# A gated feed-forward kernel on one core: the first loads in two rounds, and 256 rows of gate ahead of the later transposes

## Chip, cores, metric

One core of a Trainium2 chip. The time is that of the device for one execution, in microseconds; the profile's span runs from the first to the last instruction and is about 1.3 us shorter. A run is called slow when it is over 1.5% above the fastest of its kernel, and only the others, the fast runs, enter a ratio. All times below are counted from the first instruction of the execution, unless another start is named.

## The reference

```python
B, S, D, F = 1, 2048, 640, 1536          # all bf16
def reference(x, w_gate, w_up, w_down):
    g = silu(x @ w_gate)
    u = x @ w_up
    return (g * u) @ w_down
```

## The kernel before

The kernel gives the array (TensorE) both operands with the contracted dimension on the partitions, so x has to be transposed. Rows are worked in blocks of 512 (four chunks of 128), and the columns of gate and up in slices of 128. The first 512 rows of x are loaded as they are and transposed on the array itself, through PSUM, by an identity matrix; the other rows are transposed by a DMA, much later. Only the start of the kernel matters here.

```python
queues = (nc.sync, nc.scalar)                       # SP queue, ACT queue
halves = ((0, KD // 2 + 1), (KD // 2 + 1, KD))      # contracted chunks 0..2 on SP, 3..4 on ACT
for c in (0, 1):                                    # x: chunks 0, 1 on SP, 2, 3 on ACT
    for i, eng in enumerate(queues):
        load_x(eng, c + 2 * i, c + 2 * i + 1)
for dst, src in ((wg_sb, wg_v), (wu_sb, wu_v)):     # first slice of gate, then of up
    for eng, (k0, k1) in zip(queues, halves):
        eng.dma_start(out=dst[:, k0:k1, wslice(0, 1)], in_=src[:, k0:k1, wslice(0, 1)])
load_w(nc.sync, wg_sb, wg_v, *W_CHUNKS[1])          # next gate slice: columns 128..383
nc.scalar.activation(silu_first[:], ones[:, 0:1], ACT.Silu)     # brings the table load early
load_w(nc.sync, wu_sb, wu_v, *W_CHUNKS[1])          # next up slice
# ... all other weights, then the DMA transposes of the later rows ...
```

The loads share eight DMA semaphores (eight numbers in the trace), so the ninth load waits until one of the first eight has landed: it is issued at 2.88, just behind the landing at 2.87. The first slice is worked by itself:

```python
h = (SUB - 1) * P                                   # 384 rows
warm(N_WARM)                                        # 20 matmuls on ones
for n, c in enumerate((0, 2, 1)):
    transpose_chunk(c, [(nc.vector.tensor_copy, ("po_a", "po_b")[n % 2], 0, KD)])
transpose_chunk(SUB - 1, [(nc.vector.tensor_copy, "po_b", 0, 2), (nc.scalar.copy, "po_a", 2, KD)])
warm(2)
proj(pg, wg_sb, fc, sb, 0, h)                       # gate, 384 rows
proj(pg, wg_sb, fc, sb, h, S_BLK)                   # gate, 128 rows
proj(pu, wu_sb, fc, sb, 0, S_BLK)                   # up, 512 rows
```

`proj` is five matmuls, one for each contracted chunk of 128; `transpose_chunk` is five transposes and the copies out of PSUM. Then come silu on ScalarE and the product on VectorE, and eleven more slices in the same manner with 512 rows at a time.

Of the kernel before, what the change touches and what calls it, by code (L numbers as in the profile page):

```python
# [10 lines left out]
def _body(  # L11
# [8 lines left out]
    nc = tc.nc  # L20
    P = nc.NUM_PARTITIONS
# [5 lines left out]
    B, S0, D = x.shape  # L27
    F = w_gate.shape[1]
    S = B * S0
# [3 lines left out]
    KD = D // P  # L33
    KF = F // P
    S_BLK = 512
    NSB = S // S_BLK
    SUB = S_BLK // P
    DA = 512
    Q = 32
    N_WARM = 20  # L40
    W_CHUNKS = [(0, 1), (1, 3), (3, 6), (6, 9), (9, 12)]
    assert D % P == 0 and F % P == 0 and S % S_BLK == 0 and D > DA and SUB >= 2

    consts = ctx.enter_context(tc.tile_pool(name="consts", bufs=1))
    work = ctx.enter_context(tc.tile_pool(name="work", bufs=3))
# [8 lines left out]
    wg_sb = consts.tile([P, KD, F], bf16)  # L54
    wu_sb = consts.tile([P, KD, F], bf16)
# [7 lines left out]
    wg_v = w_gate.rearrange("(kd p) f -> p kd f", p=P)  # L63
    wu_v = w_up.rearrange("(kd p) f -> p kd f", p=P)
    wd_v = w_down.rearrange("(kf p) d -> p kf d", p=P)

    def wslice(a, b):
        return slice(a * P, b * P)

    def load_w(eng, dst, src, a, b):  # L70
        eng.dma_start(out=dst[:, :, wslice(a, b)], in_=src[:, :, wslice(a, b)])

    def load_x(eng, c0, c1):
        eng.dma_start(out=x_sb[:, c0:c1, :], in_=x_v[:, c0:c1, :])  # L74
# [4 lines left out]

    queues = (nc.sync, nc.scalar)  # L80
    halves = ((0, KD // 2 + 1), (KD // 2 + 1, KD))
    for c in (0, 1):
        for i, eng in enumerate(queues):
            load_x(eng, c + 2 * i, c + 2 * i + 1)
    for dst, src in ((wg_sb, wg_v), (wu_sb, wu_v)):
        for eng, (k0, k1) in zip(queues, halves):
            eng.dma_start(out=dst[:, k0:k1, wslice(0, 1)], in_=src[:, k0:k1, wslice(0, 1)])
    load_w(nc.sync, wg_sb, wg_v, *W_CHUNKS[1])
    nc.scalar.activation(silu_first[:], ones[:, 0:1], ACT.Silu)  # L89
    load_w(nc.sync, wu_sb, wu_v, *W_CHUNKS[1])  # L90
    for a, b in W_CHUNKS[2:]:
# [9 lines left out]
    def warm(n):  # L101
        for _ in range(n):
            nc.tensor.matmul(  # L103
                pw[:, 0:P], lhsT=ones[:], rhs=ones[:], start=True, stop=True
            )

    def keep_order(engine):

        traced = [i for i in nc.cur_bb.bb.instructions if i.engine == engine]
        for a, b in zip(traced, traced[1:]):  # L110
            tc.add_manual_dep(
                b,
                a.name,
                mybir.DependencyInfo(
                    mybir.DependencyClass.NoSync, mybir.DependencyReason.DATA
                ),
                reason="keep_order",
            )

    def transpose_chunk(c, parts):  # L120
        c_sl = slice(c * P, (c + 1) * P)
        for copy, tag, k0, k1 in parts:
            pt = psum.tile([P, k1 - k0, P], bf16, tag=tag, name="pt")
            for kd in range(k0, k1):
                nc.tensor.transpose(  # L125
                    out=pt[:, kd - k0, :],
                    in_=x_sb[:, c, kd * P : (kd + 1) * P],
                    identity=ident[:],
                )
            copy(out=xT[:, k0:k1, c_sl], in_=pt[:])  # L130

    def proj(ps, w_sb, fc, sb, c0, c1):
        for kd in range(KD):
            nc.tensor.matmul(  # L134
                ps[:, c0:c1],
                lhsT=w_sb[:, kd, fc * P : (fc + 1) * P],
                rhs=xT[:, kd, sb * S_BLK + c0 : sb * S_BLK + c1],
                start=(kd == 0),
                stop=(kd == KD - 1),
            )  # L140

    for sb in range(NSB):
        s_sl = slice(sb * S_BLK, (sb + 1) * S_BLK)
        for fc in range(KF):
            pg = psum.tile([P, S_BLK], f32, tag="gu", name="pg", bufs=4)
            pu = psum.tile([P, S_BLK], f32, tag="gu", name="pu", bufs=4)
            if sb == 0 and fc == 0:
                h = (SUB - 1) * P
                warm(N_WARM)
                for n, c in enumerate((0, 2, 1)):  # L150
                    transpose_chunk(
                        c, [(nc.vector.tensor_copy, ("po_a", "po_b")[n % 2], 0, KD)]
                    )
                transpose_chunk(
                    SUB - 1,
                    [
                        (nc.vector.tensor_copy, "po_b", 0, 2),
                        (nc.scalar.copy, "po_a", 2, KD),
                    ],
                )  # L160
                warm(2)
                proj(pg, wg_sb, fc, sb, 0, h)
                proj(pg, wg_sb, fc, sb, h, S_BLK)
                proj(pu, wu_sb, fc, sb, 0, S_BLK)
                keep_order(mybir.EngineType.PE)
                keep_order(mybir.EngineType.Activation)
            else:
                proj(pg, wg_sb, fc, sb, 0, S_BLK)
                proj(pu, wu_sb, fc, sb, 0, S_BLK)
            sg = work.tile([P, S_BLK], f32)  # L170
            nc.scalar.activation(sg[:], pg[:], ACT.Silu)  # L171
            nc.vector.tensor_tensor(  # L172
                out=aT[:, fc, s_sl], in0=sg[:], in1=pu[:], op=ALU.mult
            )


        n_t = (SUB if sb < NSB - 1 else SUB - 1) * P
        po_t = psum.tile([P, n_t], f32, tag="po_b", name="po_t")
        for kf in range(KF):
            nc.tensor.matmul(  # L180
                po_t[:],
                lhsT=wd_sb[:, kf, DA:D],
                rhs=aT[:, kf, sb * S_BLK : sb * S_BLK + n_t],
                start=(kf == 0),
                stop=(kf == KF - 1),
            )
        ot_t = outp.tile([P, n_t], bf16, name="ot_t")
        ot_q = outp.tile([P, n_t], bf16, name="ot_q")
        nc.scalar.copy(ot_t[:], po_t[:])  # L189
        nc.vector.transpose(out=ot_q[:], in_=ot_t[:])  # L190
        for q in range(P // Q):
            nc.scalar.dma_start(
                out=out2[
                    sb * S_BLK : sb * S_BLK + n_t, DA + q * Q : DA + (q + 1) * Q
                ].rearrange("(i r) c -> r i c", r=Q),
                in_=ot_q[q * Q : (q + 1) * Q, :].rearrange("r (i c) -> r i c", c=Q),
            )

        for j in range(SUB):
            s0 = sb * S_BLK + j * P  # L200
            last = sb == NSB - 1 and j == SUB - 1
            po_a = psum.tile([P, DA], f32, tag="po_a", name="po_a")
            for kf in range(KF):
                nc.tensor.matmul(  # L204
                    po_a[:],
                    lhsT=aT[:, kf, s0 : s0 + P],
                    rhs=wd_sb[:, kf, 0:DA],
                    start=(kf == 0),
                    stop=(kf == KF - 1),
                )  # L210
            ot = outp.tile([P, DA], bf16, name="ot")
            nc.scalar.copy(ot[:], po_a[:])  # L212
            nc.sync.dma_start(out=out2[s0 : s0 + P, 0:DA], in_=ot[:])
            if last:
                po_b = psum.tile([P, D - DA], f32, tag="po_b", name="po_b")
                for kf in range(KF):
                    nc.tensor.matmul(  # L217
                        po_b[:],
                        lhsT=aT[:, kf, s0 : s0 + P],
                        rhs=wd_sb[:, kf, DA:D],  # L220
                        start=(kf == 0),
                        stop=(kf == KF - 1),
                    )
                ot_b = outp.tile([P, D - DA], bf16, name="ot_b")
                nc.vector.tensor_copy(out=ot_b[:], in_=po_b[:])  # L225
                nc.scalar.dma_start(out=out2[s0 : s0 + P, DA:D], in_=ot_b[:])
# [76 lines left out]
def kernel(tc, *args):  # L303
    _body(tc, *args)
    tc.close()
    tc.compile()
    _trim(tc.nc)
# [30 lines left out]
```

## Time and profile before

| | before |
|---|---|
| time, median of 6 runs | 164.01 us (163.91 to 164.37) |
| time of the profiled execution | 164.41 us |
| span of the profiled execution | 163.1 us |
| first useful matmul (gate) | 5.39 us |
| second column slice begins | 7.56 us |

In a timeline line the columns are start, duration, engine, line of the kernel, operation, output<-inputs, shape, count, and in brackets how long the engine was idle and what ended that. In a DMA line the last number is the time from issue to landing; issue time plus that is when the waiting engine may go on. The lines are in the prediction.

### The profile page before, as it was taken

Reading aid. Unit: us, or ns where it says so; the run is one execution under the profiler, and the core shown is the slowest. Engines: PE = TensorE matmul, PEld = TensorE weight load, DVE = VectorE, ACT = ScalarE, POOL = GpSimd, SP = SyncE. Lnnn points to the kernel's source line nnn. Section 1 sums busy time; section 2 is a strip of 40 time slices with the busy share of each in tenths; the row PEclk is TensorE's granted clock in tenths of the full one; section 3 lists DMA queues with packets and bytes.
Section 4 is the critical chain, followed back from the end, with each engine's and each line's share of the span. In section 5 each row is a group of like instructions: output and inputs, shape, how many; then the busy total and the mean of one; then the engine's idle time right before and its main releaser. Section 6 shows DMA issues by size and latency. Waiting matters only on the chain.

```text
span 163.1 us, 1864 instructions
## 1 busy us (share of the span) xinstructions
PE 159.1 (98%) x764; PEld 75.2 (46%) x779; DVE 37.8 (23%) x58; ACT 42.2 (26%) x71; POOL 0.6 (0%) x6
## 2 busy tenths in 40 slices
PE   8899999999999999999999999999999999999994
PEld 7544444444444444444444444444444444445442
DVE  2323333310013333311003333331001333332000
ACT  3222222212232222221222222221214222222121
POOL 1000000000000000000000000000000000000000
DMA  7999999803200000003110000000320000000312
GB/s 212 274 333 330 361 245 187 152 6 60 67 32 0 0 0 0 4 0 34 64 64 0 2 4 0 0 0 3 62 68 32 0 0 0 0 0 4 54 34 72
DMA packets 26888, 11.26 MB, mean 69 GB/s; under 512 B 17664, under 2 KB 26880, under 8 KB 26880
## 3 DMA queue, kind: packets, MB, share of 16 engines
q1 hardware_dynamic: 17968, 10.16, 22.9%
q10 hardware_dynamic: 8912, 0.98, 3.9%
q8 instruction: 6, 0.10, 0.3%
q14 instruction: 2, 0.02, 0.0%
HBM read 6.55 MB, written 2.62 MB: 56 GB/s over the span
## 4 chain that ended last, share of the span: by engine, by line
PE 95%; DMA 2%; issue 1%; DVE 0%; SPq 0%
PE pg L134 32%; PE pu L134 31%; PE po_a L204 25%; PE po_t L180 6%; DMA x_sb<-in_x_dram 2%; PE po_b L217 0%; PE pt L125 0%; DVE xT L130 0%; SPq L74 0%; DVE ot_b L225 0%
## 5 line engine op out<-in xcount | busy, mean ns | idle before, releaser
L134 PE MATMUL pg<-xT,wg_sb 128*128 128x512 bf16 (+2 forms) x245 | 59.7, 375 | 0.2 <-DVE xT L130 0.2
L134 PE MATMUL pu<-xT,wu_sb 128*128 128x512 bf16 x230 | 59.0, 379 | 0.5
L172 DVE TENSOR_TENSOR aT<-sg,pu 128x512 bf16<-128x512 f32 x48 | 33.0, 687 | 100.8 <-PE pu L134 100.8
L171 ACT ACTIVATE sg<-pg 128x512 f32<-128x512 f32 x48 | 28.7, 597 | 71.1 <-PE pg L134 71.1
L204 PE MATMUL po_a<-wd_sb,aT 128*128 128x512 bf16 x188 | 41.9, 379 | 0.2
L134 PEld LDWEIGHTS <-wg_sb 128*128 128x128 bf16 x245 | 23.8, 98 | 28.4 <-DMA wg_sb<-in_w_gate_dram 0.4
L134 PEld LDWEIGHTS <-wu_sb 128*128 128x128 bf16 x240 | 23.4, 98 | 28.1
L204 PEld LDWEIGHTS <-aT 128*128 128x128 bf16 x192 | 18.8, 98 | 22.5
L212 ACT CAST ot<-po_a 128x512 bf16<-128x512 f32 x16 | 9.4, 585 | 32.4 <-PE po_a L204 19.2
L180 PE MATMUL po_t<-aT,wd_sb 128*128 128x512 bf16 (+1 forms) x47 | 10.3, 366 | 0.1
L180 PEld LDWEIGHTS <-wd_sb 128*128 128x128 bf16 x48 | 4.7, 98 | 5.1
L189 ACT CAST ot_t<-po_t 128x512 bf16<-128x512 f32 (+1 forms) x4 | 2.2, 558 | 11.6 <-PE po_t L180 11.6
L190 DVE STREAM_TRANSPOSE ot_q<-ot_t 128x512 bf16<-128x512 bf16 (+1 forms) x4 | 2.7, 678 | 9.1 <-ACT ot_t L189 9.1
L103 PE MATMUL pw<-ones 128*128 128x128 bf16 x22 | 2.6, 302 | 0.4 <-DVE ones L78 0.4
L225 DVE CAST ot_b<-po_b 128x128 bf16<-128x128 f32 x1 | 0.3, 292 | 9.9 <-PE po_b L217 9.9
L125 PE MATMUL pt<-ident,x_sb 128*128 128x128 bf16 x20 | 2.0, 269 | 0.5 <-DMA x_sb<-in_x_dram 0.5
L130 DVE COPY xT<-pt 128x640 bf16<-128x640 bf16 (+1 forms) x4 | 1.7, 439 | 3.5 <-PE pt L125 3.5
L103 PEld LDWEIGHTS <-ones 128*128 128x128 bf16 x22 | 2.2, 139 | 0.4 <-DVE ones L78 0.4
L125 PEld LDWEIGHTS <-x_sb 128*128 128x128 bf16 x20 | 1.6, 122 | 0.9 <-DMA x_sb<-in_x_dram 0.8
L89 ACT ACT_TABLE_LOAD x1 | 1.3, 1283 | 2.0 <-issue 2.0
L130 ACT COPY xT<-pt 128x384 bf16<-128x384 bf16 x1 | 0.5, 479 | 1.6 <-PE pt L125 1.6
L217 PEld LDWEIGHTS <-aT 128*128 128x128 bf16 x12 | 0.8, 98 | 0.2
(9 smaller groups left out, 2.1 us busy)
## 6 DMA issues: line engine op xcount, KB each, us to landing
out_dram<-ot SPq DMA_DIRECT2D x16, 128.0 KB, 1.7
wd_sb<-in_w_down_dram SPq DMA_DIRECT2D x1, 1920.0 KB, 11.8
wg_sb<-in_w_gate_dram SPq DMA_DIRECT2D x3, 480.0 KB, 7.1
wu_sb<-in_w_up_dram SPq DMA_DIRECT2D x3, 480.0 KB, 7.8
out_dram<-ot_q ACTq DMA_DIRECT2D x12, 32.0 KB, 1.9
x_sb<-in_x_dram SPq DMA_DIRECT2D x2, 160.0 KB, 3.1
x_sb<-in_x_dram ACTq DMA_DIRECT2D x2, 160.0 KB, 3.3
wg_sb<-in_w_gate_dram SPq DMA_DIRECT2D x1, 320.0 KB, 4.3
```

What stands on the lines that cost most here:

```text
L89: nc.scalar.activation(silu_first[:], ones[:, 0:1], ACT.Silu)
L103: nc.tensor.matmul(pw[:, 0:P], lhsT=ones[:], rhs=ones[:], start=True, stop=True)
L125: nc.tensor.transpose(out=pt[:, kd - k0, :], in_=x_sb[:, c, kd * P : (kd + 1) * P], identity=ident[:],)
L130: copy(out=xT[:, k0:k1, c_sl], in_=pt[:])
L134: nc.tensor.matmul(ps[:, c0:c1], lhsT=w_sb[:, kd, fc * P : (fc + 1) * P], rhs=xT[:, kd, sb * S_BLK + c0 : sb * S_BLK + c1], start=(kd == 0 ...
L171: nc.scalar.activation(sg[:], pg[:], ACT.Silu)
L172: nc.vector.tensor_tensor(out=aT[:, fc, s_sl], in0=sg[:], in1=pu[:], op=ALU.mult)
L180: nc.tensor.matmul(po_t[:], lhsT=wd_sb[:, kf, DA:D], rhs=aT[:, kf, sb * S_BLK : sb * S_BLK + n_t], start=(kf == 0), stop=(kf == KF - 1),)
L189: nc.scalar.copy(ot_t[:], po_t[:])
L190: nc.vector.transpose(out=ot_q[:], in_=ot_t[:])
L204: nc.tensor.matmul(po_a[:], lhsT=aT[:, kf, s0 : s0 + P], rhs=wd_sb[:, kf, 0:DA], start=(kf == 0), stop=(kf == KF - 1),)
L212: nc.scalar.copy(ot[:], po_a[:])
```

## The change

The intent is to use the array's early pauses. x and the first weight slices come in two rounds, (chunks 0 and 1, gate slice), then (chunks 2 and 3, up slice), each round split over both queues. While the second round is on its way, gate is worked for the first 256 rows. The next gate slice is split over both queues too, which lets its SP half be issued earlier.

```diff
-    N_WARM = 20
+    N_WARM = 17
+    N_GAP = 2
...
-    for c in (0, 1):
-        for i, eng in enumerate(queues):
-            load_x(eng, c + 2 * i, c + 2 * i + 1)
-    for dst, src in ((wg_sb, wg_v), (wu_sb, wu_v)):
+    def load_halves(dst, src, a, b):
         for eng, (k0, k1) in zip(queues, halves):
-            eng.dma_start(out=dst[:, k0:k1, wslice(0, 1)], in_=src[:, k0:k1, wslice(0, 1)])
-    load_w(nc.sync, wg_sb, wg_v, *W_CHUNKS[1])
+            eng.dma_start(out=dst[:, k0:k1, wslice(a, b)], in_=src[:, k0:k1, wslice(a, b)])
+
+    for c, dst, src in ((0, wg_sb, wg_v), (SUB // 2, wu_sb, wu_v)):
+        for i, eng in enumerate(queues):
+            load_x(eng, c + i, c + i + 1)
+        load_halves(dst, src, *W_CHUNKS[0])
+    load_halves(wg_sb, wg_v, *W_CHUNKS[1])
...
-                h = (SUB - 1) * P
+                h = SUB // 2 * P
+                dve, act = nc.vector.tensor_copy, nc.scalar.copy
                 warm(N_WARM)
...                (the four transposes in a row, warm(2), gate on 384 rows: removed)
+                transpose_chunk(0, [(dve, "po_a", 0, KD)])
+                transpose_chunk(1, [(dve, "po_b", 0, KD)])
+                warm(N_GAP)
+                proj(pg, wg_sb, fc, sb, 0, P)
+                proj(pg, wg_sb, fc, sb, P, h)
+                for c in (2, 3):
+                    transpose_chunk(c, [(act, "po_a", 0, 2), (dve, "po_b", 2, KD)])
+                proj(pu, wu_sb, fc, sb, 0, h)
                 proj(pg, wg_sb, fc, sb, h, S_BLK)
-                proj(pu, wu_sb, fc, sb, 0, S_BLK)
+                proj(pu, wu_sb, fc, sb, h, S_BLK)
```

More of the change, by code (lines that the diff above doesn't have):

```diff
@@ L39, in _body @@
     Q = 32
-    N_WARM = 20
+    N_WARM = 17
+    N_GAP = 2
     W_CHUNKS = [(0, 1), (1, 3), (3, 6), (6, 9), (9, 12)]
-    assert D % P == 0 and F % P == 0 and S % S_BLK == 0 and D > DA and SUB >= 2
+    assert D % P == 0 and F % P == 0 and S % S_BLK == 0 and D > DA and SUB == 4
     consts = ctx.enter_context(tc.tile_pool(name="consts", bufs=1))
@@ L81, in _body @@
     halves = ((0, KD // 2 + 1), (KD // 2 + 1, KD))
-    for c in (0, 1):
+    def load_halves(dst, src, a, b):
+        for eng, (k0, k1) in zip(queues, halves):
+            eng.dma_start(out=dst[:, k0:k1, wslice(a, b)], in_=src[:, k0:k1, wslice(a, b)])
+    for c, dst, src in ((0, wg_sb, wg_v), (SUB // 2, wu_sb, wu_v)):
         for i, eng in enumerate(queues):
-            load_x(eng, c + 2 * i, c + 2 * i + 1)
-    for dst, src in ((wg_sb, wg_v), (wu_sb, wu_v)):
-        for eng, (k0, k1) in zip(queues, halves):
-            eng.dma_start(out=dst[:, k0:k1, wslice(0, 1)], in_=src[:, k0:k1, wslice(0, 1)])
-    load_w(nc.sync, wg_sb, wg_v, *W_CHUNKS[1])
+            load_x(eng, c + i, c + i + 1)
+        load_halves(dst, src, *W_CHUNKS[0])
+    load_halves(wg_sb, wg_v, *W_CHUNKS[1])
     nc.scalar.activation(silu_first[:], ones[:, 0:1], ACT.Silu)
@@ L147, in _body @@
             if sb == 0 and fc == 0:
-                h = (SUB - 1) * P
+                h = SUB // 2 * P
+                dve, act = nc.vector.tensor_copy, nc.scalar.copy
                 warm(N_WARM)
-                for n, c in enumerate((0, 2, 1)):
-                    transpose_chunk(
-                        c, [(nc.vector.tensor_copy, ("po_a", "po_b")[n % 2], 0, KD)]
-                    )
-                transpose_chunk(
-                    SUB - 1,
-                    [
-                        (nc.vector.tensor_copy, "po_b", 0, 2),
-                        (nc.scalar.copy, "po_a", 2, KD),
-                    ],
-                )
-                warm(2)
-                proj(pg, wg_sb, fc, sb, 0, h)
+                transpose_chunk(0, [(dve, "po_a", 0, KD)])
[6 more added lines that the diff above has]
+                proj(pu, wu_sb, fc, sb, 0, h)
                 proj(pg, wg_sb, fc, sb, h, S_BLK)
-                proj(pu, wu_sb, fc, sb, 0, S_BLK)
+                proj(pu, wu_sb, fc, sb, h, S_BLK)
                 keep_order(mybir.EngineType.PE)
```

## The prediction

> **What bounds the kernel now.** I read the page first (busy shares, then the chain that ended last), then the start of the timeline, then the DMA issues with their time to landing, then stretches of the start. From the page:
>
> ```profile
> PE 159.1 (98%) x764; PEld 75.2 (46%) x779; DVE 37.8 (23%) x58; ACT 42.2 (26%) x71; POOL 0.6 (0%) x6
> ...
> PE 95%; DMA 2%; issue 1%; DVE 0%; SPq 0%
> PE pg L134 32%; PE pu L134 31%; PE po_a L204 25%; PE po_t L180 6%; DMA x_sb<-in_x_dram 2%; PE po_b L217 0%; PE pt L125 0%; DVE xT L130 0%; SPq L74 0%; DVE ot_b L225 0%
> ```
>
> The chain is TensorE for 95% of the span, and 2% (3.8 us) is one load of x. The change touches nothing but the start, so it can only buy what lies before the array runs without gaps. The timeline of the start shows where that is:
>
> ```profile
> 0.40 2.31 PE L103 MATMUL pw<-ones 128*128 128x128 bf16 x20 [0.40 <-DVE ones L78]
> ...
> 2.51 1.27 PE L125 MATMUL pt<-ident,x_sb 128*128 128x128 bf16 x10
> ...
> 3.28 1.02 DVE L130 COPY xT<-pt 128x640 bf16<-128x640 bf16 x2 [2.94 <-PE pt L125]
> ...
> 4.31 0.78 PE L125 MATMUL pt<-ident,x_sb 128*128 128x128 bf16 x10 [0.53 <-DMA x_sb<-in_x_dram]
> ...
> 5.39 1.25 PE L134 MATMUL pg<-xT,wg_sb 128*128 128x384 bf16 x10 [0.19 <-DVE xT L130]
> ...
> 6.70 1.03 PE L134 MATMUL pu<-xT,wu_sb 128*128 128x512 bf16 x4
> ...
> 7.56 1.24 PE L134 MATMUL pg<-xT,wg_sb 128*128 128x512 bf16 x5
> ```
>
> Two chunks of x are transposed from 2.51, the other two only from 4.31, and the first useful matmul starts at 5.39. From there the array has no gap (one of the five pu records is missing: the first pu must have begun near 6.48, one 0.216 step before 6.70). I take 7.56, the start of the second column slice, as my measuring point: what moves it moves the end, as everything after it is dense TensorE work and identical in both kernels.
>
> Which loads hold that start? The DMA view:
>
> ```profile
> wg_sb<-in_w_gate_dram SPq DMA_DIRECT2D x1, 320.0 KB, 4.3
> wu_sb<-in_w_up_dram SPq DMA_DIRECT2D x1, 320.0 KB, 4.8
> wg_sb<-in_w_gate_dram SPq DMA_DIRECT2D x1, 96.0 KB, 4.4
> wu_sb<-in_w_up_dram SPq DMA_DIRECT2D x1, 96.0 KB, 4.9
> ...
> wg_sb<-in_w_gate_dram ACTq DMA_DIRECT2D x1, 64.0 KB, 4.5
> wu_sb<-in_w_up_dram ACTq DMA_DIRECT2D x1, 64.0 KB, 4.5
> ```
>
> Added to the issue times of the timeline, the landings are: the four chunks of x at 2.46 and 2.87 (the first two issued), 4.26 and 4.48; the first gate slice at 0.91 + 4.4 = 5.33 and 5.51; the first up slice at 1.39 + 4.9 = 6.26 (SP half) and 1.52 + 4.5 = 6.04 (ACT half); the next gate slice at 2.88 + 4.3 = 7.19, the next up slice at 8.12. So at 5.39 the last x chunks and the gate slice came almost together, and up was in at 6.26, before its use at 6.48. Before the second slice the margin is small: 7.19 for a use at 7.56, 8.12 for a use at 8.64.
>
> The last view is the load's rate by stretch (GB/s is the last column):
>
> ```profile
> 1.00:2.00 1.00, 1.00 (x13) 1.00 (x11) 0.00 (x0) 0.00 (x0) 0.00 (x0) 1.00 0.85 223
> 2.00:3.00 1.00, 1.00 (x12) 0.94 (x11) 0.00 (x0) 0.96 (x1) 0.00 (x0) 1.00 1.03 361
> 3.00:4.00 1.00, 0.78 (x8) 0.51 (x5) 0.68 (x2) 0.53 (x2) 0.00 (x0) 1.00 1.06 266
> 4.00:4.50 0.50, 0.19 (x3) 0.20 (x4) 0.30 (x1) 0.00 (x0) 0.00 (x0) 1.00 0.86 195
> 4.50:5.40 0.90, 0.71 (x13) 0.55 (x12) 0.56 (x2) 0.28 (x1) 0.00 (x0) 1.00 0.71 194
> ```
>
> x and both first slices are 640 + 160 + 160 KB = 983 thousand bytes. By 4.5 the rows sum to 223 + 361 + 266 + 97 = 947. So nearly all of it has moved by 4.5, yet up counts as landed only at 6.26: a few late DMA engines hold each semaphore. The rate falls between 4.0 and 5.4, because the next gate slice is issued only at 2.88, after the second landing.
>
> **What the Trainium skill says.** "DMA: Bandwidth & Descriptors", section "Issuing engines are not separate DMA queues": loads from both queues share the same 16 engines, so splitting saves issue time only. The trace agrees so far: x from two queues runs at 361 GB/s together. Reordering therefore shifts who lands first, not when all has landed. The same page, "Why a DMA increments its semaphore by 16 and not by 1": a load is complete only when each of its engines is. That fits 947 of 983 moved at 4.5 and landings up to 6.26. "TensorE: Matmul & The Clock Gate", "Back-to-back issue gap": 107 ns per 128-column matmul cold, about 56 warm, 216 for 512 columns. The trace agrees: 20 warm-ups in 2.31 us with a 0.31 us tail are 105 ns apart; five 512-column matmuls take 1.08 us in the chain. "ScalarE: Activation LUTs", "What ACT_TABLE_LOAD costs": 1283 ns; the page's row has 1283.
>
> **The change part by part.**
> Warm-ups, 20 to 17: they end near 0.40 + 17 x 0.107 = 2.2, before x lands at 2.46. Worth nothing.
> Chunks 0 and 1 first, one from each queue: they take the places of today's first two, so land at 2.46 and 2.87; transposes 2.51 to 3.57 as now, copies done at 3.77 and 4.31 as now (3.28, then 3.81 plus 0.49).
> Gate slice in second place instead of third: about 328 thousand bytes of x at about 361 GB/s, 0.9 us, no longer lie ahead of it. It lands at 5.33 - 0.9 = 4.4, perhaps before 4.
> Gate on 256 rows: two times five 128-column matmuls, 5 x 0.107 + 5 x 0.056 to 0.107, so 0.8 to 1.1 us, from about 4.3 (3.8 at best): done near 5.1. This is the work that moves into today's idle time.
> Transposes of chunks 2 and 3: they wait for x in third place. It was 4.26 and 4.48; with the 164 thousand bytes of gate ahead (0.7 us at some 230 GB/s) about 4.9 to 5.1. Ten at 0.056 are 0.56, done at about 5.7; copies in two engines, 0.3 to 0.4 each, done about 6.1, beside the next matmuls.
> Then up on rows 0 to 255, gate on 256 to 511, up on 256 to 511: 15 matmuls of 256 columns, each half of 0.216, so 15 x 0.109 = 1.64 us. All of it stands behind the up slice, and that is still the last of the same 983 thousand bytes. I see no reason for it to land before about 6.0 to 6.3. The second half of the next gate slice now even comes from the other queue and can interleave with it.
> The table load moves behind the fifth load of the ACT queue, whose issue waits for the first ACT landing (2.87): about 3.4 to 4.7 plus 0.2 for the small activation, done before its first copy at about 5.1.
> The next gate slice: SP half issued after x lands at 2.46 instead of 2.87, so 0.4 us earlier and into the slack after 4.0; lands about 6.7. The up slice behind it at about 7.7.
>
> Sum at the measuring point. With nothing waiting for up: 5.3 + 3 x 0.55 = 6.95, a gain of 0.6. With up at 6.26: 6.3 + 1.64 = 7.95, a loss of 0.4. Break-even is up landing at 7.56 - 1.64 - 0.05 = 5.87. Today only 1.08 us of matmul stand behind up; after the change 1.64 do. The change lifts the early wait and makes the later one dearer.
>
> **The rivals.**
> First, the gain holds (-0.4 to -0.6, 163.5 to 163.6). For it: most engines finish the up slice long before 6.26, so with fewer late engines the wait is gone; and warm-up counts cut to fit the landing look like a start that was tuned on the chip. Against: nothing in the change shortens the loads.
> Second, up is the new wait (+0.2 to +0.5, 164.3 to 164.5). For it: 983 thousand bytes either way and 0.56 us more work behind the last of them. Against: the late landing may be one execution's accident.
> Third, gain at the start, given back at the second slice: gate at 7.19 or up at 8.12 would cap the gain at about 0.3 (163.75). The earlier issue speaks against it.
> Fourth, the late table load delays ACT's copy of chunk 2, and with it the second gate half, by some 0.3 us; hidden if up is late anyway.
>
> **Range and chances.** I give the gain somewhat over half, as the late engines vary and the order of first loads may favour it, and the up wait most of the rest: 0.55 x -0.45 + 0.35 x 0.35 + 0.10 x 0 is about -0.1, so 163.95 us against 164.06. Eight in ten: 163.35 to 164.6. 2% would be 3.3 us, and the whole idle time from 2.5 to 5.4 is less than that: within 2% has 0.98.
>
> **What would show it.** Right: the first gate matmul near 3.8 to 4.4, of 128 columns; the first 256-column up matmul starting just after the up slice lands, with an idle in front of it put down to wu_sb; the second slice at 6.95 to 7.95 instead of 7.56, and the time shifted by the same. Wrong: the gate slice landing no earlier than 5; the up wait at zero with the second slice still late; any change of matmul spacing after the second slice; a gap in front of the second gate slice.

## The result

| | before | changed |
|---|---|---|
| median of 6 runs | 164.01 us | 164.76 us (164.41 to 164.90) |
| ratio, 95% interval | 1 | 1.0038 (1.0024 to 1.0053) |
| span of the profiled execution | 163.1 us | 163.5 us |
| first useful matmul | 5.39 us | 3.85 us |
| second column slice begins | 7.56 us | 7.97 us |

A ratio is the mean time of one kernel's fast runs over that of the other's of the same rounds, so it is not quite the ratio of the medians. The change is within 2%, and clearly slower: 0.38% is 0.62 us. The prediction stood at 163.95 us with a gain as the likelier outcome; the kernel lost instead.

The page of the changed kernel still has the array on nearly the whole chain, with more of a load in it than before:

```profile
PE 96%; DMA 3%; SPq 0%; DVE 0%; issue 0%
PE pu L137 32%; PE pg L137 31%; PE po_a L203 25%; PE po_t L179 6%; DMA x_sb<-in_x_dram 3%; PE pt L128 1%; PE po_b L216 0%; SPq L85 0%; SPq L75 0%; DVE ot_b L224 0%
```

Its timeline of the start (VectorE, ScalarE and queue lines left out):

```profile
2.55 1.25 PE L128 MATMUL pt<-ident,x_sb 128*128 128x128 bf16 x10 [0.16 <-DMA x_sb<-in_x_dram]
...
3.85 1.23 PE L137 MATMUL pg<-xT,wg_sb 128*128 128x128 bf16 x10
...
5.23 1.25 PE L128 MATMUL pt<-ident,x_sb 128*128 128x128 bf16 x10 [0.15 <-DMA x_sb<-in_x_dram]
...
6.27 0.77 PE L137 MATMUL pu<-xT,wu_sb 128*128 128x256 bf16 x5
...
6.88 0.71 PE L137 MATMUL pg<-xT,wg_sb 128*128 128x256 bf16 x5
...
7.43 0.71 PE L137 MATMUL pu<-xT,wu_sb 128*128 128x256 bf16 x5
...
7.97 1.24 PE L137 MATMUL pg<-xT,wg_sb 128*128 128x512 bf16 x5
```

The gate work did move forward, from 5.39 to 3.85. But the late transposes start at 5.23, not at 4.31. They take 1.25 us where the same ten took 0.78 in before: the array is still at half clock. (In a line of ten, the duration is nine steps and one whole operation; the steps are 0.104 us here and 0.062 there.) The trace's records of the granted clock have full speed from 6.39 on; in before, the spacing of the matmuls falls to 0.056 us near 4.5. And no load stands before the first up matmul at 6.27: it follows the transposes directly.

The DMA view shows the loads behind this:

```profile
x_sb<-in_x_dram SPq DMA_DIRECT2D x2, 160.0 KB, 3.4
x_sb<-in_x_dram ACTq DMA_DIRECT2D x2, 160.0 KB, 3.6
...
wg_sb<-in_w_gate_dram SPq DMA_DIRECT2D x1, 96.0 KB, 3.0
wu_sb<-in_w_up_dram SPq DMA_DIRECT2D x1, 96.0 KB, 4.6
```

The gate slice lands at 0.45 + 3.0 = 3.4 instead of 5.3, the up slice at 1.44 + 4.6 = 6.0 instead of 6.3. The lines for x are medians of two. The last line of the view of the tile x_sb has the extremes, here for before and then for the changed kernel:

```profile
DMA to landing us min/median/max: 2.5/3.3/3.9
```

```profile
DMA to landing us min/median/max: 2.5/3.6/4.4
```

The last chunk of x was issued at 0.56 + 3.9 = 4.48 in before, and lands at 1.04 + 4.4 = 5.45 in the changed kernel: 1 us later. The second slice moved by 0.41 us, the span by 0.43, so the loss of the profiled pair is all in this start.

Two theories followed. **Load theory:** the second x pair, now behind the gate slice, lands late, and 2.2 us of array work (0.56 of transposes and 1.64 of matmuls at full clock) stand behind it. **Clock theory:** 17 warm-ups leave a hole before the first transpose (2.18 to 2.55), the array gets full clock 2 us later, and the loss is work done at half speed. A third, from the prediction: not x but the up slice holds it. In this one trace up was in at 6.00, before the transposes ended, but experiment 4 comes back to it.

### The profile page after: what moved, and what is told of

The parts are those of the page before. It is cut to its first block, busy times and chain, and to the rows that moved or that the text cites. A ratio compares the mean times of both kernels' runs of the same rounds, so it can differ in the third digit from the quotient of the medians.

```text
span 163.5 us, 1895 instructions
## 1 busy us (share of the span) xinstructions
PE 160.7 (98%) x786; PEld 76.7 (47%) x786; DVE 37.9 (23%) x58; ACT 42.5 (26%) x72; POOL 0.6 (0%) x6
## 3 DMA queue, kind: packets, MB, share of 16 engines
HBM read 6.55 MB, written 2.62 MB: 56 GB/s over the span
## 4 chain that ended last, share of the span: by engine, by line
PE 96%; DMA 3%; SPq 0%; DVE 0%; issue 0%
PE pu L137 32%; PE pg L137 31%; PE po_a L203 25%; PE po_t L179 6%; DMA x_sb<-in_x_dram 3%; PE pt L128 1%; PE po_b L216 0%; SPq L85 0%; SPq L75 0%; DVE ot_b L224 0%
## 5 line engine op out<-in xcount | busy, mean ns | idle before, releaser
L137 PE MATMUL pu<-xT,wu_sb 128*128 128x512 bf16 (+1 forms) x245 | 59.9, 375 | 0.0
L137 PEld LDWEIGHTS <-wg_sb 128*128 128x128 bf16 x250 | 24.6, 100 | 27.6
L137 PEld LDWEIGHTS <-wu_sb 128*128 128x128 bf16 x245 | 24.0, 98 | 27.8
L128 PE MATMUL pt<-ident,x_sb 128*128 128x128 bf16 x20 | 2.5, 311 | 0.3 <-DMA x_sb<-in_x_dram 0.3
L92 ACT ACT_TABLE_LOAD x1 | 1.3, 1283 | 3.4 <-DMA x_sb<-in_x_dram 3.4
L133 ACT COPY xT<-pt 128x256 bf16<-128x256 bf16 x2 | 0.7, 372 | 0.9 <-PE pt L128 0.9
```

The lines of the kernel that those rows point to most:

```text
L128: nc.tensor.transpose(out=pt[:, kd - k0, :], in_=x_sb[:, c, kd * P : (kd + 1) * P], identity=ident[:],)
L133: copy(out=xT[:, k0:k1, c_sl], in_=pt[:])
L137: nc.tensor.matmul(ps[:, c0:c1], lhsT=w_sb[:, kd, fc * P : (fc + 1) * P], rhs=xT[:, kd, sb * S_BLK + c0 : sb * S_BLK + c1], start=(kd == 0 ...
```

## The experiments

### 1. The number of warm-ups

The changed kernel with 20 (a_warm20), and the kernel before with 17 (b_warm17); nothing else is touched.

```diff
-    N_WARM = 17
+    N_WARM = 20
```

> The changed kernel with 20 first warm-ups in place of 17, nothing else. Clock theory (the 0.36 us hole between the last of 17 warm-ups at 2.18 and the first transpose at 2.55 puts off the full clock, granted only at 6.39 in the changed kernel's trace): full clock back at about 4.4, the ten late transposes at 0.056 instead of 0.107, so 0.3 to 0.5 us faster than the changed kernel, ratio to before 1.001 to 1.002. Load theory (the second x pair landing at 5.19 and 5.45 instead of 4.26 and 4.48 sets the loss): no change, ratio 1.003 to 1.005.

> The kernel before with 17 first warm-ups in place of 20, nothing else. Clock theory: the same hole of 0.36 us appears, full clock comes some 2 us later, so the late transposes and the first gate group run cold: slower by 0.3 to 0.7 us, ratio 1.002 to 1.004. Load theory: ratio 1.000 within 0.001.

Measured, beside before at 164.45 us (11 runs, this chip): a_warm20 164.87 us, ratio 1.0024 (1.0008 to 1.0040); b_warm17 164.35 us, ratio 0.9993 (0.9972 to 1.0015). The interval of a_warm20 overlaps that of the changed kernel, so a small part of the loss may be recovered, but it isn't shown. The profile of a_warm20 says more:

```profile
5.48 0.73 PE L128 MATMUL pt<-ident,x_sb 128*128 128x128 bf16 x10 [0.53 <-DMA x_sb<-in_x_dram]
6.36 0.72 PE L137 MATMUL pu<-xT,wu_sb 128*128 128x256 bf16 x5
...
8.01 1.24 PE L137 MATMUL pg<-xT,wg_sb 128*128 128x512 bf16 x5
```

This execution had full clock from 3.88 (its clock records), the late transposes take 0.73 us, and yet the second slice begins at 8.01, no earlier than in the changed kernel: x landed at 5.43 and 5.71 and the up slice at 6.31. And b_warm17 had the hole and a late clock (near 6.0, where its 384-row matmuls go from 0.32 us apart to 0.16) without a loss in its median; only its profiled execution, at 164.76 one of the longest of its six runs, starts the second slice at 7.91. The clock theory as the whole cause is in doubt; it is not yet tested cleanly, as each profile shows one execution with its own moment of full clock.

### 2. Load order and work order apart

The change has two halves that can be had one at a time. b_loads_after is the kernel before with the loads of the changed one; a_loads_before is the work order of the changed kernel (17 warm-ups) with the loads of before.

```diff
 b_loads_after: in the kernel before
+    for c, dst, src in ((0, wg_sb, wg_v), (SUB // 2, wu_sb, wu_v)):
+        ...                                   (loads as in the change)
-                for n, c in enumerate((0, 2, 1)):
+                for n, c in enumerate((0, 1, 2)):
 a_loads_before: in the changed kernel
+    for c in (0, 2):
+        for i, eng in enumerate(queues):
+            load_x(eng, c + i, c + i + 1)
+    ...                                       (gate and up halves, next gate slice on SP)
```

> The order of work of before (all four chunks transposed, then gate, then up) under the loads of the changed kernel; 20 warm-ups. Load theory: the last x chunk lands at about 5.2 to 5.45 instead of 4.26 to 4.48, the first gate matmul starts at about 6.3 instead of 5.39 and the second slice at about 8.4 instead of 7.56: slower by 0.7 to 0.9 us, ratio 1.004 to 1.006. Clock theory: the loads cost little by themselves, ratio below 1.002.

> The order of work of the changed kernel (256 rows of gate ahead of the late transposes; 17 warm-ups) under the loads of before (all x first, then gate, then up; next gate slice on one queue). Load theory: x is in at about 4.3 to 4.5, the gate slice only at 5.3 to 5.5, so 256 rows of gate wait until 5.4 and 1.1 to 1.6 us of transposes and more follow: slower than before, ratio 1.003 to 1.006, about as slow as the changed kernel. Theory that 1.64 us of matmul behind the up slice is the loss: the same ratio, 1.003 to 1.005. Clock theory: full clock late as in the changed kernel, first 512-column gate matmul at 8 or later.

Measured beside the same runs of before: b_loads_after 166.25 us, ratio 1.0094 (1.0061 to 1.0126); a_loads_before 164.79 us, ratio 1.0027 (0.9994 to 1.0059). Both scatter far more than before does (165.27 to 168.53, and 164.36 to 166.85). The longest run of each counts as slow and is in the median but not in the ratio; without it the medians are 166.16 and 164.63 and the ranges end at 166.83 and 166.02. The loads alone are the costly half, more than was expected; the work order alone is not shown to cost anything. The profile of b_loads_after mixes both theories, with x landing at 5.09 and full clock only at 8.61. Its second slice starts at 9.48, 1.92 us after that of before; had it followed the landing of x by 3.08 us as in before, it would start at 8.17, so by this estimate some 1.3 us of the 1.92 are cold matmuls. It doesn't separate them. One thing more tells against the clock theory as it was put: a_loads_before has the same 17 warm-ups and the same hole (its first transpose is at 2.54), and its clock records have full speed from 4.16. The hole does not by itself set the moment of full clock.

### 3. The same four, with the clock taken out: a first try that failed

To take the clock out, the first loads were held back behind a chain of VectorE operations, while warm-ups bring the array to full clock.

```diff
+    ones2 = consts.tile([P, P], bf16)
+    slow = consts.tile([P, 3, 1024], f32)
+    nc.vector.memset(slow[:], 1.0)
+    for _ in range(9):
+        nc.vector.tensor_tensor(out=slow[:, 0, :], in0=slow[:, 1, :], in1=slow[:, 2, :], op=ALU.mult)
+    nc.vector.tensor_copy(out=ones2[:], in_=ones[:])
+    nc.vector.tensor_copy(out=x_sb[:, :, 0:1], in_=...)     # the loads of x wait for this
...
-                warm(N_WARM)
+                warm(100)
+                warm(40, ones2)                             # these wait for it too
...
+                keep_order(mybir.EngineType.SP)
+                keep_order(mybir.EngineType.DVE)
```

pb is the kernel before held back, pa the changed kernel, pb_la and pa_lb the two mixed ones.

> The kernel before with its loads held back some 9 to 10 us by a chain of VectorE operations, while 100 warm-ups bring the array to full clock, and 40 more warm-ups from the moment the loads are released. All comparisons are between the four held-back kernels; each is some 10 us (6%) slower than before by construction. In this one: transposes at 0.056 us, gate on all rows starting about 5.0 to 5.3 after the first load's issue, the second column slice about 7.2 to 7.5 after it.

> The changed kernel, held back in the same way, so that the clock can play no part. Clock theory (the whole loss of 0.6 us is a clock that comes late): equal to the held-back kernel before or faster, -0.3 to 0.1 us. Load and work theory (the second x pair and the up slice land late and 1.6 us of matmul stand behind them): 0.3 to 0.6 us slower than the held-back kernel before, the second slice about 7.7 after the first load's issue.

> Held back: the order of work of before under the loads of the changed kernel. Load theory: x complete 1 us later, so 0.9 to 1.2 us slower than the held-back kernel before. Clock theory: the 1.5 us of the same pair without holding back was cold matmuls, and under 0.3 us of it is left.

> Held back: the order of work of the changed kernel under the loads of before. Load theory: gate slice in at about 5.0, then 0.55 gate, 0.55 transposes, 1.64 for the rest: second slice at about 7.6 to 7.8, 0.1 to 0.4 us slower than the held-back kernel before, and faster than the held-back changed kernel. Theory that the work behind up is the loss: as slow as the held-back changed kernel, since both have 1.64 us behind up.

Measured medians: pb 180.02, pa 180.18, pb_la 180.63, pa_lb 179.68 us (ratios to before 1.0953, 1.0954, 1.0989, 1.0934, intervals of about 0.0025 on either side). The design was at fault. The chain took 14.9 us (the memset 2.62 us, each multiplication 1.23), the 100 warm-ups were over by 8.4, and after the pause the clock records of pb have half speed again, from 12.07 to 18.90. The 40 warm-ups then ran cold, over 4.1 us instead of 2.2, and stood in front of the transposes in pb, pa and pb_la. The times therefore decide nothing. What the four profiles do give is four more sets of landing times.

### 4. The same four, mended

```diff
-    for _ in range(9):
+    for _ in range(5):
-                warm(100)
-                warm(40, ones2)
+                warm(118)
+                warm(44, ones2)
```

> The held-back kernel before again, mended: in the first try the chain of VectorE operations took 14.9 us and the array fell idle for 7 us and went back to half clock. Now five operations (loads released at about 10 us), 118 warm-ups before and 44 after the release, so the array is at full clock and nearly without a pause when x lands. Second column slice 7.2 to 7.5 us after the first load's issue. Comparisons between the four held-back kernels only.

> The changed kernel, held back the mended way. Clock theory (the loss is a late clock): equal to the held-back kernel before within 0.15 us, or faster. Load theory: second x pair lands about 5.3 after the first issue instead of about 3.8 to 4.4, second slice at about 7.6 to 7.8, 0.2 to 0.5 us slower than the held-back kernel before.

> Held back the mended way: order of work of before, loads of the changed kernel. Load theory: gate starts when the late x pair is transposed and copied, 5.4 + 1.1, plus 2.17: second slice at about 8.6, 0.9 to 1.3 us slower than the held-back kernel before. Clock theory: under 0.3 us slower.

> Held back the mended way: order of work of the changed kernel, loads of before. Load theory: gate slice at 4.7 to 5.3, then 0.55 + 0.55 + 1.64: second slice at 7.4 to 8.0, within 0.3 us of the held-back kernel before on either side. Theory that the 1.64 us of work behind the up slice is the loss: as slow as the held-back changed kernel.

| held back, at full clock | loads of before | loads of the change |
|---|---|---|
| work order of before | pb2 174.48 us, 1.0604 (1.0577 to 1.0630) | pb_la2 175.89 us, 1.0729 (1.0684 to 1.0773) |
| work order of the change | pa_lb2 174.50 us, 1.0614 (1.0591 to 1.0636) | pa2 175.09 us, 1.0645 (1.0621 to 1.0670) |

The ratios are to the unheld kernel before of the same rounds (164.39 us); they are compared with one another. From pb2 to pa2 the medians differ by 0.61 us, which is the loss of the change (0.62 by the ratio), with the array at 0.056 us per 128-column matmul throughout its start. The intervals of these two overlap a little, so the size is rough. By the medians the loads alone cost 1.4 us, well outside the noise, the work order alone 0.02, and with the loads of the change the new work order wins back 0.8 of the 1.4. The clock theory as the only cause falls: the loss is there without it. The 1.64 us of work behind the up slice are not the loss by themselves either, because pa_lb2 has as much of them as pa2; whether they cost when up is late too, as in pa2, these four don't separate.

The timelines say where it happens. First pb2 and pa_lb2, with the loads of before (the first load is issued at 9.96 in each of the four, within 0.02):

```profile
14.85 1.25 PE L145 MATMUL pg<-xT,wg_sb 128*128 128x384 bf16 x10
15.94 1.24 PE L145 MATMUL pu<-xT,wu_sb 128*128 128x512 bf16 x5
17.24 1.25 PE L145 MATMUL pg<-xT,wg_sb 128*128 128x512 bf16 x5
```

```profile
14.71 0.80 PE L146 MATMUL pg<-xT,wg_sb 128*128 128x128 bf16 x10 [0.76 <-DMA wg_sb<-in_w_gate_dram]
15.36 0.72 PE L137 MATMUL pt<-ident,x_sb 128*128 128x128 bf16 x10
...
17.55 1.24 PE L146 MATMUL pg<-xT,wg_sb 128*128 128x512 bf16 x5
```

then pb_la2 and pa2, with the loads of the change:

```profile
15.48 0.73 PE L138 MATMUL pt<-ident,x_sb 128*128 128x128 bf16 x10 [1.82 <-DMA x_sb<-in_x_dram]
...
18.69 1.24 PE L147 MATMUL pg<-xT,wg_sb 128*128 128x512 bf16 x5
```

```profile
15.20 0.73 PE L139 MATMUL pt<-ident,x_sb 128*128 128x128 bf16 x10 [0.32 <-DMA x_sb<-in_x_dram]
15.98 0.72 PE L148 MATMUL pu<-xT,wu_sb 128*128 128x256 bf16 x5
...
17.63 1.24 PE L148 MATMUL pg<-xT,wg_sb 128*128 128x512 bf16 x5
19.31 1.25 PE L148 MATMUL pu<-xT,wu_sb 128*128 128x512 bf16 x5 [0.44 <-DMA wu_sb<-in_w_up_dram]
```

In pb_la2 the array sits idle for 1.82 us until x is there; in pa2 the gate work fills that gap and the idle before the transposes is down to 0.32. That is the part which the change had right. In pa2 the first up matmul at 15.98 does stand just behind the up slice, which landed at about 15.9. There is one more loss: the second slice starts 0.39 after that of pb2, but its up half waits for the next up slice and starts 0.96 after that of pb2 (19.31 against 18.35).

Two cautions go with this. First, the medians are not the start alone. Counted at the up half of the second slice, the profiles put pa_lb2 0.28, pa2 0.96 and pb_la2 1.42 behind pb2. But from there to the end the profiled execution of pb2 takes some 0.5 us longer than those of pa2 and pa_lb2, mostly a pause of the array at 48.8 in the down projection, behind a late copy on ScalarE (pb_la2 has 0.2 of it). How many of the other runs have that pause isn't known. So the 0.02 of the work order and the 0.8 won back are those of whole runs; at the start the profiles show 0.28 lost and 0.46 won back.

Second, x is not always the last thing waited for. In pa2 the last transpose starts at 15.72, and the up matmul 0.27 later, when up is in (15.94). The same is so in two executions at full clock that were not held back: a_warm20 (last transpose 5.99, up in at 6.31, up matmul 6.36) and a_gate1_again of experiment 5 (5.93, 6.14 and 6.18):

```profile
5.41 0.73 PE L128 MATMUL pt<-ident,x_sb 128*128 128x128 bf16 x10 [0.47 <-DMA x_sb<-in_x_dram]
6.18 0.72 PE L137 MATMUL pu<-xT,wu_sb 128*128 128x256 bf16 x5
```

In these three, with x in time, the up slice alone would have held the second slice where it was. What is shown is that the changed loads cost; which of their late landings is the last differs from execution to execution.

### 5. Why the second x pair is late

The trace has one semaphore event for each of the 16 DMA engines of a load. Counted from the issue of the first load, for the later half of the second x pair:

| | traces | median engine (ninth of 16), mean | last engine, mean | last engine, range |
|---|---|---|---|---|
| pair sent directly behind the first | 9 | 3.72 | 4.10 | 3.87 to 4.48 |
| gate slice sent between the pairs | 10 | 4.57 | 5.47 | 4.68 to 5.86 (nine of them 5.09 or later) |

So 0.85 us of the shift is in the median engine, and the last engine falls behind the median one by 0.90 instead of 0.38. For the first there are two readings that no run separates: the 164 thousand bytes ahead (an estimate of 0.7 us at 230 GB/s), and the load being issued 0.48 us later (1.04 against 0.56), behind one more issue on its queue, which took 0.45 us. For the second, three causes were tried: the split next gate slice (a_gate1_one), the table load that this split delays (a_table_early), and the rows of 256 bytes of the slice ahead (b_wd_ahead, where as many bytes of w_down in longer rows take that place). The same round had a version that was meant to beat both kernels (best).

```diff
 a_gate1_one
-    load_halves(wg_sb, wg_v, *W_CHUNKS[1])
+    load_w(nc.sync, wg_sb, wg_v, *W_CHUNKS[1])
 a_table_early
-    load_halves(wg_sb, wg_v, *W_CHUNKS[1])
     nc.scalar.activation(silu_first[:], ones[:, 0:1], ACT.Silu)
+    load_halves(wg_sb, wg_v, *W_CHUNKS[1])
 b_wd_ahead (on b_loads_after)
+    nc.sync.dma_start(out=wd_sb[:, 0, 0:384], in_=wd_v[:, 0, 0:384])        # between the x pairs
+    nc.scalar.dma_start(out=wd_sb[:, 0, 384:D], in_=wd_v[:, 0, 384:D])
     ...                                       (gate and up slices after the second pair)
 best (on a_loads_before; N_WARM 21, N_GAP 6)
     transpose chunks 0, 1; warm(N_GAP); transpose chunks 2, 3
+    proj(pg, wg_sb, fc, sb, 0, h)
+    proj(pg, wg_sb, fc, sb, h, S_BLK)
+    proj(pu, wu_sb, fc, sb, 0, S_BLK)
```

> The changed kernel with the next gate slice (columns 128 to 383) as one load on the SP queue, as before; the table load of ScalarE then returns to about 2.05 us by itself. If the split load or the table load delays the second x pair: its later half completes at 4.4 to 4.9 instead of 5.1 to 5.9, and the ratio to before falls to 1.000 to 1.002. If the bytes or rows ahead of it delay it: 5.1 to 5.9 as in the changed kernel, ratio 1.002 to 1.005.

> The changed kernel with the small activation, and so the table load, ahead of the ACT half of the next gate slice: table load at about 2.05 us, that half issued at about 3.5. If the table load at 3.43 to 4.71 is what holds DMA engines: the second x pair completes at 4.4 to 4.9. If not: 5.1 to 5.9 and a ratio to before of 1.002 to 1.005.

> Order of work of before; in second place, between the two x pairs, not the gate slice but as many bytes (164 thousand) of w_down in rows of 768 and 512 bytes; gate and up slices after x, up after a wait for a free semaphore, so the time itself will be worse and is not the question. Bytes theory: the later half of the second x pair completes at 5.1 to 5.9 as in the changed kernel. Row-size theory: the bytes pass at 300 GB/s and more, the pair completes about 0.5 us later than under the loads of before, at 4.4 to 4.8, with at most one late engine.

> Loads of before; 21 warm-ups, transposes of the first two chunks, 6 warm-ups in the pause, transposes of the last two with copies shared by ScalarE and VectorE, then gate on 256 rows, gate on the other 256, up on all 512. Load theory: with x at 3.9 to 4.5 and gate at 4.7 to 5.5 the second slice starts at 7.1 to 7.6, so 0 to 0.4 us faster than before, ratio 0.9975 to 1.000, and 0.6 to 1.0 us faster than the changed kernel. Clock theory: the same, as fewer pauses bring the full clock earlier; this run does not tell the two apart.

Measured, beside before at 164.16 us:

| | median | ratio | second pair lands |
|---|---|---|---|
| a_gate1_one | 164.70 us | 1.0032 (1.0006 to 1.0057) | 4.30 and 4.68 |
| a_table_early | 166.00 us | 1.0104 (1.0084 to 1.0125) | 5.44 and 5.62 |
| b_wd_ahead (2 runs) | 167.17 us | 1.0176 (1.0145 to 1.0206) | 5.51 and 5.70 |
| best | 164.29 us | 1.0003 (0.9983 to 1.0023) | 3.44 and 3.97 |

The table load was at 2.05 in a_table_early, and x was late all the same: it is not the table load. In b_wd_ahead the bytes came in long rows, and x was late all the same, in the one trace of it: the short rows are not needed for this. a_gate1_one was in time, alone of all, but a second profile of the same program was needed to tell cause from chance, and with it the split was put into the kernel before by itself:

```diff
 b_gate1_split: in the kernel before
-    load_w(nc.sync, wg_sb, wg_v, *W_CHUNKS[1])
+    for eng, (k0, k1) in zip(queues, halves):
+        eng.dma_start(out=wg_sb[:, k0:k1, wslice(*W_CHUNKS[1])], in_=wg_v[:, k0:k1, wslice(*W_CHUNKS[1])])
```

> The same program as a_gate1_one, for a second profile. If splitting the next gate slice is what holds engines back in the second x pair: its later half again at 4.4 to 4.9. If it was chance: 5.1 to 5.9 as in the other traces under these loads. The ratio to before 1.001 to 1.005 as the first time.

> The kernel before with only the next gate slice split over both queues (the table load moves behind its ACT half, as in the changed kernel). If the split costs by itself: x still at 3.9 to 4.5, but gate or up slice late (up past 6.3) or a wait at the second slice, ratio 1.001 to 1.004. If it costs nothing: ratio 0.999 to 1.001, the second gate slice landing 0.2 to 0.4 us earlier than 7.19.

Beside before at 164.04 us: a_gate1_again 164.70 us, ratio 1.0042 (1.0029 to 1.0055), and now x lands at 5.37 and 5.54. So the timely x of a_gate1_one was chance, not the unsplit load. That execution teaches something else: x was in at 4.68 and up at 5.38, and still it took 164.83 us.

```profile
4.90 1.27 PE L128 MATMUL pt<-ident,x_sb 128*128 128x128 bf16 x10
5.97 1.07 PE L137 MATMUL pu<-xT,wu_sb 128*128 128x256 bf16 x5
```

The array was at half clock (full from 6.71 by the records), and the second slice began near 7.97, where it does in the changed kernel. So a late clock is enough for the same loss in a single execution with timely loads, and outside the held-back kernels the two shares of it are not separated. b_gate1_split: 164.24 us, ratio 1.0010 (0.9991 to 1.0029); x at 3.37 and 3.91. Its next gate slice came at 6.33 and 6.46, 0.7 us earlier than in before, but its next up slice at 8.72, and the array waited for that:

```profile
7.38 1.24 PE L135 MATMUL pg<-xT,wg_sb 128*128 128x512 bf16 x5
8.76 1.25 PE L135 MATMUL pu<-xT,wu_sb 128*128 128x512 bf16 x5
```

Back to back the second line would start at 8.46. In a_table_early the split did harm openly: its ACT half, issued at 3.68, landed at 9.76, and the array waited for it in the middle of the gate group (1.13 us idle). The version best ties with before. Its profile has x at 3.97, gate at 4.75 and the second slice at 7.78, because the late transposes and half of gate ran at half clock.

What stays open is what holds one to seven engines back by 0.5 us and more once a slice is sent between the pairs. That it comes with the place in the order is shown by 9 traces against 10 of 11 (b_wd_ahead counted); the mechanism is not.

## Why the prediction was wrong

- **The step that failed** is the first rival, which got over half of the weight: "most engines finish the up slice long before 6.26, so with fewer late engines the wait is gone". The late engines stayed. Up had to land before 5.87 to break even; it landed at 6.00 in the profile, and more than 5.87 after the first load's issue in eight of the ten traces with these loads. The second x pair had late engines as well (5.45 for a last landing of about 5.1), and the second slice began at 7.97.
- **The sum behind that gain** left the x pair out. It starts the 1.64 us of matmuls at 5.3, while the text before it has the transposes, which stand ahead of them, done at about 5.7. With that figure the best case is 5.7 + 1.64 = 7.34, a gain of 0.2 and not 0.6. Measured were 6.27 and 7.97: the transposes began about 0.1 later than the 5.1 told, took 1.04 instead of 0.56, and the rest took 1.70.
- **The measuring point** held in this pair: the second slice moved 0.41 us and the span 0.43. But the trace behind it was of an execution of 164.41 us, where the median is 164.01. Its last x chunk at 4.48 is the latest of nine traces with that load order, and its up slice at 6.26 too (the others 5.38 to 5.79). So the loss reads 0.4 us in the pair of profiles and 0.62 in the runs. The prediction took one long execution for the kernel.
- **Warm-ups worth nothing:** right as far as the runs resolve (0.9993 and 1.0024, experiment 1).
- **Gate slice in second place:** right in direction, and better than told: 3.41 and 3.60, where 4.4, perhaps before 4, was expected. Gate on 256 rows at 3.85 as in the best case told.
- **The second x pair** is the term of the sum that was too small. "With the 164 thousand bytes of gate ahead (0.7 us at some 230 GB/s) about 4.9 to 5.1": it was 5.19 and 5.45 in the profile, and the later half averaged 1.37 us behind that of the other order. The 0.7 told for the bytes compares with 0.85 in the median engine; a last engine that trails by 0.52 more was not told. Part of this was hidden in the estimate, because it started from an execution whose last engine was late already (4.48, where the mean is 4.10).
- **"Ten at 0.056 are 0.56"** failed in the profile: they took ten steps of 0.104 at half clock. The held-back kernels show that the loss is there without this, so it is not the only cause; in the profiled execution it is where the time went (1.04 us from the first late transpose to the first up matmul).
- **The up slice as the new wait:** the second rival named the right direction and a nearly right size (0.2 to 0.5), but in the profiled execution no wait for up is seen, so its 7.95 against the 7.97 measured is luck there. At full clock the wait is there as told, in pa2, a_warm20 and a_gate1_again. Its landing, "before about 6.0 to 6.3" being unlikely, came true too: with the loads of the change the later half came at 5.38 to 6.36 (mean 6.05, ten traces). Only the base was off: with the loads of before it was 5.38 to 6.26 with a mean of 5.63 (nine traces), so the up slice moved back as well.
- **What it drew from the skill:** from "Issuing engines are not separate DMA queues" it inferred that reordering "shifts who lands first, not when all has landed". The page doesn't say that, and the last landing of the same bytes moved from 5.63 to 6.05 in the mean. The 361 GB/s it gives as agreement don't show shared engines either; no run loads x from one queue. The issue gaps of 56 and 216 ns are those which "Back-to-back issue gap" gives for single matmuls; for a stream with weight loads the same section has 81 and 131 ns, and the trace here, which is such a stream, has 56 and 216.
- **1.64 us for the rest** was right (6.27 to 7.97 is 1.70, the first step still cold), and so were the next gate slice (6.7 told, 6.71 and 6.92 measured) and the table load (3.43 to 4.71, harmless).
- **The next up slice** "at about 7.7" landed at 8.56, and in pa2 it cost the array 0.44 us of idle. The third rival was waved away on this.
- **The weights:** the sum itself needed up before 5.87 to break even, and the text saw no reason for that; it still gave the gain more than half, on the guess that so careful a change had been tuned on the chip. That guess was not a reading of the profile.

## What to carry to other kernels

When several small loads compete at a start, ask for each what is still to be done after it, and send the one with the longest tail of work first: here 2.2 us of array work stood behind the second x pair, and putting a slice before it cost more than the work brought forward won back. That is one kernel's case, not a rule. Count on the slowest DMA engine as the traces show it, not only on bytes over bandwidth, and look at more than one execution: the profiled one may be off the median by as much as the change is worth. To judge a load order apart from the array's clock, hold the loads back until the clock is up, and check in the trace that it stayed up.

## What the Trainium skill lacked or had wrong

- "TensorE: Matmul & The Clock Gate", "What's actually happening", puts full clock after some 3.4 us of sustained work, with a variation of 500 ns. Here it came at 3.88, 4.16, 6.39, 6.71, 8.61 and 9.73 us in six kernels that all began warm-ups at 0.4; the late ones had up to 1.8 us of pauses. The page's remark that the window runs free may fit this, though no run here shows it; its remark that the ramp costs under 1% of a typical span doesn't help where 0.4% is the question.
- "ScalarE: Activation LUTs", "What ACT_TABLE_LOAD costs", adds about 1380 ns of drain to the 1283 ns of a table load. In the changed kernel the load ran from 3.43 to 4.71 and the next activation started at 4.73, without such a drain. It is the kernel's first table load; a switch between two sets, of which the page speaks, is in no run here.
- "DMA: Bandwidth & Descriptors", "Why a DMA increments its semaphore by 16 and not by 1", says that all engines must be in, but no page says how far the last one trails: 0.38 us behind the median in one order of loads, 0.90 in the other.
- The same page, "Issuing engines are not separate DMA queues", says that splitting saves issue time only. No page warns that the half on the second queue can trail far: 9.76 against 7.36 us for the two halves of one slice in a_table_early, issued at 3.68 and 3.13.
